# A new written-out order, split first projections and query weights loaded first, in a one-core attention and MLP block

## Chip, cores, metric

The kernel runs on one core of one Trainium2 chip. The metric is the device time in microseconds (us) of one execution. One execution was also taken with the hardware profiler; every start, duration and wait below comes from that one.

## What is computed

A transformer block over 2048 tokens of width 640. Cut to what matters:

```python
h  = x + A(layernorm(x))          # A: 32 heads of 20, in 4 segments of 512 tokens
h2 = h + B(layernorm(h))          # B: 640 -> 1728, silu, 1728 -> 640

# A, per head and segment s:
p     = softmax(q_s k_s^T * 20**-0.5 + causal mask)
a_dot = p v_s
phi   = lambda t: where(t > 0, t + 1, exp(t))
a_mem = phi(q_s) M / (phi(q_s) z + 1e-6)      # memory of the segments before s
o     = sigmoid(beta) * a_mem + (1 - sigmoid(beta)) * a_dot
M, z  = M + phi(k_s)^T v_s,  z + sum(phi(k_s))
return concat(o) @ wo
```

## The kernel before

All data lies in on-chip memory as bf16; the matrix results go to eight banks of the accumulator `ps_all`. The 32 heads are taken four at a time, in eight groups `g`; four heads of 20 rows stand at rows 0, 32, 64 and 96, and the 12 rows left between them hold the other heads, so that five projection blocks `c` (0 to 4) of 128 columns carry all of q and all of k. Groups 5 to 7 are copied out of the gaps by small transfers (`vt`, L841).

The program is a graph of named tasks, and **each task's place is written out by hand** in one long string, `ORDER`. `schedule` goes through it word by word; a word is a name, an engine after a slash where there is a choice (A ScalarE, D VectorE, S the SyncE queue), and after a colon the buffer slots that the task takes. Every engine then executes its own tasks strictly in that order, so a word that is late holds up everything behind it on its engine. Semaphore waits are derived from what each task reads and writes. Names used below:

| word | task | line | engine |
|---|---|---|---|
| `x0`.., `w_q`, `w_k`, `w_wv`, `w_w1_0`.. | load tokens or a weight | 562, 565 | SyncE or ScalarE queue |
| `n1_st`, `n1_rs`, `n1_ap` | statistics, 1/std, normalize a block of 128 tokens | 703, 712, 720 | VectorE, GpSimd, VectorE |
| `n1_tp`, `n1_te` | transpose by matmul (segment 0), its copy to `xT` | 729, 738/739 | TensorE, ScalarE/VectorE |
| `n1_tr`, `n2_tr` | transpose by DMA (later segments, and `hT`) | 744 | SyncE queue |
| `fillN` | N matmuls on zeros into an unused bank | 597 | TensorE |
| `v si`, `ve si` | values of block i in segment s, copy to `Vx` | 771, 781/782 | TensorE, ScalarE/VectorE |
| `re_wq c`, `re_wk c` | rearrange block c of a loaded weight | 675/677 | ScalarE/VectorE |
| `pr s c w`, `qe s c w` | projection c of q (w=0) or k (w=1), copy to `QK` | 805, 813/814 | TensorE, ScalarE/VectorE |
| `ex`, `ph` | exp and phi of q or k | 820, 827/830 | ScalarE, VectorE |
| `qk..`, `e..`, `mk..` | scores, their exp (two banks each), causal mask | 877, 888, 900 | TensorE, ScalarE, GpSimd |
| `av`, `oe`, `tn`, `nm`, `ad` | weights times values, copy, transpose back with the memory term, normalize, add | 923, 936/938, 952/956, 969 to 989, 997 | |
| `kt`, `mz`, `ma`, `mb` | the memory M and z | 1037, 1045, 1070 to 1081 | |
| `ot`, `wo`, `rs` | transpose the output, times wo, residual | 1098, 1106, 1114 | |
| `h1`, `th`, `s`, `h2`, `o`, `out` | MLP, second residual, store | 1130, 1138, 1144, 1162, 1172, 1176 | |

In segment 0 the first 256 tokens are scored first (`qk0x0` to `qk7x0`, two blocks), then the other 256 (`ya`, `yb`); later segments go in ticks of one group. Segment 0's MLP is in two halves, the later ones are in one.

At the start the four token blocks come in on the SyncE queue, and the three attention weights, 800 KB each, on ScalarE's queue, in the order `wv`, `wq`, `wk`. One ScalarE operation, `warm`, stands ahead of them in `ORDER`. The values take `VS = 21` columns per head, 20 and one column of ones; that constant is the same before and after.

Of the kernel before, what the change touches and what calls it, by code (L numbers as in the profile page):

```python
# [11 lines left out]
PE, AC, DV, PO, SP = "pe", "act", "dve", "pool", "sp"  # L12
# [312 lines left out]
D = 640  # L325
# [22 lines left out]
SPLIT0 = ()  # L348
# [10 lines left out]
zpad:0 warm w_wv:0 w_q:0 w_k x0:0 x1:1 x2:2 x3:3 beta mt0 mta0 mtb0 epsc iota halfc vpad1 epsg0 n1_st0:0 sel  # L359
n1_st1:2 mt1 n1_rs0 n1_ap0:0 n1_rs1 fill38:0 n1_tp0:0 n1_st2:1 n1_ap1:0 fill10:2 n1_tp1:2 n1_st3:3 n1_te0/A:0 n1_rs2  # L360
n1_rs3 n1_ap2:0 fill2:4 v00:0 n1_tp2:4 n1_ap3:1 n1_tp3:6 n1_te1/A n1_te2/D re_wq1/D:0 v01:2 n1_te3/A pr010:6 lsc0
re_wq2/D re_wk1/D:0 re_wk0/D pr011:4 re_wq0/D mt2 qe010/D:0 ve00/A:0 re_wq3/A re_wk4/D re_wk2/A pr001:0 qe001/D:0
x4/A:4,5,6,7 qe011/A zf0 ex011:0 ve01/D qk1x0:4 re_wk3/D re_wq4/D n1_st4:3 e1x0:0 pr000:1 e1x2 pr021:0 pr020:2 vpad0
lsc1 mk1x lsc2 lsc3 qe000/A qe021/A:0 ex001:1 qk0x0:4 qe020/A e0x2:1 e0x0 pr041:0 pr030:2 ex021:2 n1_st5:1 n1_st7:2
qe030/D:0 ph001:0 ph011:1 qe041/A:0 mk0x qk2x0:4 av1x:1 oe1x/D:0 e2x0:0 e2x2 pr031:3 qe031/A pr040:2 qk3x0:4 av0x:0
tn1x:1 qe040/A e3x0:1 e3x2 n1_rs5 n1_rs4 n1_rs7 v02:2 qk0yb0:4 oe0x/D:1 nm1x:0,0 n1_st6:0 ve02/D n1_ap7:1 v03:0 mt3
mta3 n1_ap5:0 mta1 mk2x n1_rs6 mk3x ve03/D ex031:0 e0yb0:0 e0yb2 fill1:2 qk1yb0:4 x8/S:8,9,10,11 w_w1_4/S:0 av2x:2
oe2x/D:0 e1yb0:1 e1yb2 w_w2_3/S:0 vt03:0 vt09 fill5:3 qk4x0:0 vt06 w_w2_0/S e4x2:0 e4x0 qk0ya0:4 e0ya0:0 e0ya2 vt00
kt00:0 w_w1_0/S vt05 vt07 vt011 vt010 vt02 n1_tr5:0 tn2x:0 v11:2 qk1ya0:4 n1_ap6:2 ph021:0 n1_tr6 vt01 vt08 ve11/A:1
n1_st8:0 n1_ap4:0 nm2x:0 av3x:0 e1ya2:1 e1ya0 v12:2 vt04 oe3x/D:0 ve12/A mk4x tn3x:0 nm3x:0 mk0yb av4x:1 n1_rs8  # L370
mk1yb qk5x0:4 n1_tr4 tn0x:0 e5x2:0 e5x0 mk5x n1_tr7 v10:2 qk6x0:4 n1_st9:3 nm0x:0 oe4x/A:1 e6x0:1 v13:0 e6x2 ve10/D
av5x:2 qk7x0:4 ve13/D kt02:1 oe5x/D:0 w_wo/S:0 ex041:2 e7x0:0 e7x2 av1y:3 mz02:0 tn5x:2 mk6x av6x:1 qk2yb0:4
ma02/A:0 e2yb0:1 e2yb2 tn4x:0 mtb1 mk7x oe1y/D:0 oe6x/A:1 nm5x:0 pr101:3 fill1:2 qk2ya0:4 e2ya2:1 e2ya0 tn6x:1
pr130:2 mm5 mk2yb mm2 qe101/D:0 nm4x:0 tn1y:0 nm6x:1 av7x:1 av0y:3 oe0y/A:0 qk3ya0:4 e3ya0:0 e3ya2 w_w2_2/S kt01:1
w_w1_1/S ph031:1 oe7x/D:1 w_w1_2/S w_w1_3/S nm1y:1 tn7x:1 nm7x:0 av2y:3 pr100:0 qk3yb0:4 n1_st11:1 n1_st10:2
oe2y/A:1 qe100/D e3yb2:1 e3yb0 ot1:0 ot0 w_w2_4/S mz01:1 pr111:3 qk4ya0:4 qe130/A:0 ma01/D:1 wo1:0 e4ya0:1 e4ya2
ph041:0 kt04:1 w_w2_1/S qe111/D:0 tn2y:3 rs1 n2_st1:4 mk3yb av3y:2 oe3y/A:1 qk4yb0:4 e4yb0:1 e4yb2 nm2y:0 n2_rs1
wo0:0 ex100:2 qk5ya0:4 tn3y:3 e5ya0:0 e5ya2 rs0 n2_st0:6 mk4yb n2_ap1:1 n2_rs0 pr121:2 mz04:0 nm3y:0 n2_ap0:0
ma04/A:2 mz00:1 qk5yb0:4 av4y:0 oe4y/D:1 ma00/D:3 e5yb0:0 e5yb2 pr141:3 qk6ya0:4 tn0y:1 ex101:0 ex111:1 n2_tr1:0
n2_tr0 pr140:0 qe141/D:0 zf1 n1_rs9 qe121/D:0 nm0y:0 e6ya2:1 e6ya0 mk5yb av5y:3 tn4y:2 n1_rs11 h1_0_6_0:1 qe140/D  # L380
ph100:0 ph111:0 oe5y/A:1 th0_6_0:0 qk6yb0:4 e6yb0:0 e6yb2 h1_0_4_0:0 pr110:3 mta2 mtb2 mzc2 mm4 s0_6_0:0 mm0 mk6yb
n1_rs10 th0_4_0:1 ex121:1 qk7ya0:4 s0_4_0 pr120:1 h1_0_1_0:0 e7ya0:0 e7ya2 nm4y:0 n1_ap9:0 h1_0_3_0:2 qe110/D
th0_1_0:1 qe120/D s0_1_0 qk7yb0:4 th0_3_0:0 h1_0_9_0:1 h1_0_11_0:0 e7yb2:1 h1_0_5_0:3 s0_3_0 th0_9_0:0 e7yb0 s0_9_0
av6y:1 qk8a0:4 th0_11_0:0 th0_5_0:1 oe6y/A:0 h1_0_0_0:2 tn6y:1 s0_5_0 epsg1 s0_11_0 e8a2:1 nm6y:0 th0_0_0:0
h1_0_7_0:3 e8a0 s0_0_0 n1_ap11:1 th0_7_0:0 h1_0_2_0:0 h1_0_13_0:1 mm9 mzc9 mzc0 qk8e0:4 mtb3 mm11 mk7yb av7y:2
s0_7_0 th0_13_0:1 s0_13_0 oe7y/D:0 e8e2:0 e8e0 h1_0_8_0:3 pr131:1 h1_0_12_0:2 th0_2_0:1 s0_2_0 qk8b0:4 th0_8_0:0
qe131/A th0_12_0:1 ph121:2 s0_8_0 n1_ap10:2 s0_12_0 h2_0_0:0 h1_0_10_0:3 h2_0_1 ex120:2 n1_ap8:3 kt03:0 n1_tr9:0
vt11:0 n1_tr11 vt16 n1_tr8 vt18 mk8a mk8e e8b0:1 e8b2 qk9a0:4 mm7 mk8b mzc11 mm3 mzc3 mm1 mzc1 th0_10_0:1 h2_0_2
tn5y:2 e9a0:0 s0_10_0 h2_0_3 e9a2 mk9a mb00:0 nm5y:0 qk9b0:4 o0 ph101:1 e9b2:0 e9b0 h2_1_0:2 av8:0 tn7y:1 qk10a0:4
oe8/A:1 e10a0:1 e10a2 nm7y:0 h2_1_1 tn8:0 h2_1_2 ph120:0 qk10b0:4 nm8:0,0 h2_1_3 vt12 vt110 vt111 kt10:1 vt19 vt10  # L390
ot3 ex141:2 e10b0:1 e10b2 o1 mk9b mm10 mzc10 mb04:0 mz03:0 ma03/D:4 qk10e0:4 ex131:0 e10e2:1 e10e0 av9:2 ph131:1 mm8
mk10b mzc7 mb01:0 mk10a mk10e ex110:0 oe9/D:1 wo3:0 qk11a0:4 e11a2:0 e11a0 mk11a mzc4 rs3 v20:2 av10:0 qk11b0:4
e11b2:1 ph110:0 ve20/D:0 e11b0 vt17 vt14 ot2 kt12:0 vt15 vt13 n1_tr10 oe10/D:0 ex130:0 mzc5 mk11b wo2:2 tn9:0
qk12a0:4 rs2 pr220:2 e12a2:1 e12a0 av11:3 qk13a0:4 oe11/A:1 nm9:0,1 pr211:0 e13a2:0 e13a0 pr200:3 qk12b0:4 ex140:1
# [59 lines left out]
def build(nc, es, A_x, A_wq, A_wk, A_wv, A_wo, A_beta, B_x, B_w1, B_w2, out):  # L454
# [109 lines left out]
    def load_w(k, dst, src, prio, bw, wr, kind="plain", engs=(SP, AC)):  # L564
        dma("w_" + k, [(W["wk"], [0])] if kind == "plain" else [], wr, lambda e: e.dma_start(out=dst, in_=src), prio, bw, kind, engs=engs)
# [666 lines left out]
```

## Time and profile before

| | |
|---|---|
| runs of the kernel before | 316.68, 314.07, 317.78, 314.02 us; median 315.37 |
| the profiled execution | 316.68 us; first to last instruction 314.9 us |
| TensorE busy | 298.2 us (95%), 2864 matmuls |
| ScalarE busy | 228.0 us (72%) |
| VectorE busy | 221.2 us (70%) |
| GpSimd busy | 144.5 us (46%) |
| DMA | 24.56 MB, mean 78 GB/s |
| granted TensorE clock, mean | 0.995 |
| matmuls on zeros (L597) | 57, 8.9 us busy |
| last matmul ends | 311.8 us |

Busy time of an engine is the union of its instructions' times. The granted clock is the share of full speed at which TensorE was allowed to run. The profiled execution's own time lies 1.78 us above its span, for what lies before the first and after the last instruction.

### The profile page before, as it was taken

What the parts mean: (1) busy time and instruction counts of PE and PEld (TensorE: products, weight loads), DVE (VectorE), ACT (ScalarE), POOL (GpSimd) and SP (SyncE); (2) the same over time, 40 slices, a digit from 0 to 9 for tenths busy, and PEclk for the clock granted to TensorE, in tenths of its full rate; (3) what the DMA queues carried; (4) which work ended last, traced back from release to release, by engine and by line L of the source; (5) the groups of instructions that cost most, each with busy time, mean ns of one, the idle gap of its engine ahead of it and who ended that gap; (6) DMA issues with size and microseconds to landing.
All of it is one profiled execution on the core that took longest, in us unless ns stands there. A gap on an engine that the chain in (4) does not pass through costs nothing.

```text
span 314.9 us, 7209 instructions
## 1 busy us (share of the span) xinstructions
PE 298.2 (95%) x2864; PEld 165.2 (52%) x2891; DVE 221.2 (70%) x489; ACT 228.0 (72%) x322; POOL 144.5 (46%) x280
## 2 busy tenths in 40 slices
PE   8799899999999989999979999999999999999995
PEld 6534454547555445565534545556554456654553
DVE  3869568777578997798879984647977495826422
ACT  3488889999899989979779998976888850005300
POOL 4328542574556773573628546434774540300000
PEclk9999799999999999999999999999999999999999
DMA  7487477440444020045563220066040004221013
GB/s 248 153 292 196 83 217 194 110 60 2 77 75 73 17 44 19 1 73 113 107 63 108 51 60 0 2 104 60 1 86 2 0 2 85 62 42 65 0 44 125
DMA packets 48353, 24.56 MB, mean 78 GB/s; under 512 B 38848, under 2 KB 47232, under 8 KB 48320
## 3 DMA queue, kind: packets, MB, share of 16 engines
q1 hardware_dynamic: 45824, 20.99, 31.0%
q10 hardware_dynamic: 2496, 3.11, 2.9%
q8 instruction: 23, 0.38, 0.5%
q14 instruction: 10, 0.08, 0.1%
HBM read 10.33 MB, written 2.62 MB: 41 GB/s over the span
## 4 chain that ended last, share of the span: by engine, by line
PE 67%; DVE 12%; ACT 10%; DMA 8%; issue 2%; POOL 0%; SPq 0%; ACTq 0%; DVEq 0%
PE ps_all L1162 18%; PE ps_all L1130 18%; PE ps_all L805 7%; PE ps_all L877 6%; PE ps_all L1106 6%; PE ps_all L923 4%; DMA x_tok<-in_A_x_dram 4%; ACT PTB L888 4%; PE ps_all L771 4%; ACT PTA L888 3%; DMA hT<-xn_rot 3%; DVE stt L703 2%; PE ps_all L952 2%; DVE xn_rot L720 1%; DVE phiQ L830 1%
## 5 line engine op out<-in xcount | busy, mean ns | idle before, releaser
L1130 PE MATMUL ps_all<-hT,w_sb 128*128 128x512 bf16 (+3 forms) x340 | 65.3, 336 | 4.0 <-DVE phiQ L827 1.8
L1162 PE MATMUL ps_all<-w_sb,sT 128*128 128x320 bf16 (+1 forms) x448 | 68.2, 300 | 0.1
L888 ACT ACTIVATE PTA<-ps_all 128x1024 bf16<-128x1024 f32 x64 | 62.2, 1026 | 6.7 <-PE ps_all L877 6.5
L1138 ACT ACTIVATE th<-ps_all 128x512 f32<-128x512 f32 (+3 forms) x70 | 34.5, 518 | 43.0 <-PE ps_all L1130 34.9
L888 ACT ACTIVATE PTB<-ps_all 128x1024 bf16<-128x1024 f32 (+1 forms) x64 | 59.0, 973 | 6.1 <-PE ps_all L877 6.0
L1144 DVE SCALAR_TENSOR_TENSOR sT<-th,ps_all 128x512 bf16<-128x512 f32 (+3 forms) x70 | 38.9, 575 | 29.9 <-ACT th L1138 29.1
L900 POOL TENSOR_SCALAR_AFFINE_SELECT PTB<-PTB 128x512 bf16<-128x512 bf16 x64 | 41.6, 650 | 34.8 <-ACT PTB L888 32.6
L1162 PEld LDWEIGHTS ps_all<-w_sb,sT 128*128 128x128 bf16 (+1 forms) x448 | 40.4, 97 | 24.4 <-issue 8.1
L1130 PEld LDWEIGHTS ps_all<-hT,w_sb 128*128 128x128 bf16 (+1 forms) x350 | 31.6, 99 | 30.6 <-issue 5.1
L888 ACT ACTIVATE PTE<-ps_all 128x1024 bf16<-128x1024 f32 (+1 forms) x40 | 35.5, 939 | 3.0 <-PE ps_all L877 2.1
L900 POOL TENSOR_SCALAR_AFFINE_SELECT PTE<-PTE 128x512 bf16<-128x512 bf16 x40 | 25.8, 646 | 21.7 <-ACT PTE L888 20.3
L703 DVE BATCH_NORM_STATS2 stt<-x_tok 128x6 f32<-128x320 bf16 x64 | 28.1, 480 | 5.9 <-DMA x_tok<-in_A_x_dram 5.5
L900 POOL TENSOR_SCALAR_AFFINE_SELECT PTA<-PTA 128x512 bf16<-128x512 bf16 x24 | 15.7, 655 | 25.3 <-ACT PTA L888 25.3
L1172 DVE SCALAR_TENSOR_TENSOR x_tok<-ps_all,x_tok 128x640 bf16<-128x640 f32 x16 | 13.2, 823 | 18.1 <-PE ps_all L1162 18.0
L771 PE MATMUL ps_all<-wv_sb,xT 128*128 128x320 bf16 x160 | 25.6, 309 | 0.2
L997 POOL TENSOR_TENSOR otok<-on 128x320 bf16<-128x320 bf16 x24 | 19.3, 810 | 11.8 <-DVE on L989 11.8
L805 PE MATMUL ps_all<-xT,wqr 128*128 128x512 bf16 x92 | 23.2, 379 | 1.5 <-issue 0.6
L1106 PE MATMUL ps_all<-wo_sb,oT 128*128 128x320 bf16 x160 | 23.9, 299 | 0.1
L805 PE MATMUL ps_all<-xT,wkr 128*128 128x512 bf16 x91 | 23.0, 380 | 0.7 <-issue 0.3
L814 DVE CAST QK<-ps_all 128x512 bf16<-128x512 f32 x24 | 16.1, 679 | 10.3 <-PE ps_all L805 10.3
L877 PE MATMUL ps_all<-QK 20*128 20x256 bf16 (+3 forms) x360 | 20.8, 288 | 2.6 <-ACT PTB L888 1.3
L712 POOL TENSOR_TENSOR rst<-mvt,eps_c 128x1 f32<-128x1 f32 x32 | 6.9, 217 | 32.0 <-DVE mvt L706 29.5
(78 smaller groups left out, 415.5 us busy)
## 6 DMA issues: line engine op xcount, KB each, us to landing
out_dram<-x_tok SPq DMA_DIRECT2D x16, 160.0 KB, 2.0
w_sb<-in_B_w_dram SPq DMA_DIRECT2D x5, 432.0 KB, 4.3
w_sb<-in_B_w_dram SPq DMA_DIRECT2D x3, 480.0 KB, 5.7
x_tok<-in_A_x_dram SPq DMA_DIRECT2D x2, 640.0 KB, 5.7
QKV<-QK SPq DMA_DIRECT2D x16, 72.0 KB
wv_sb<-in_A_wv_dram ACTq DMA_DIRECT2D x1, 800.0 KB, 5.4
sT<-in_A_wq_dram ACTq DMA_DIRECT2D x1, 800.0 KB, 8.8
sT<-in_A_wk_dram ACTq DMA_DIRECT2D x1, 800.0 KB, 10.3
```

Source lines behind the costliest of these rows:

```text
L703: T.add(DV, lambda e, hh=hh: e.bn_stats(out=stt[:, s, 6 * hh:6 * hh + 6], in_=xb[:, 320 * hh:320 * hh + 320]), reads=R((xa, xsub)), writes ...
L771: fns.append(lambda e, c=c, hh=hh: e.matmul(bank(ps, hh)[:, 0:320], lhsT=xT[:, c, 128 * i:128 * i + 128], rhs=wv_sb[:, c, 320 * hh:320 * h ...
L805: fns = [lambda e, kc=kc: e.matmul(bank(ps)[:, lo:hi], lhsT=wt[:, kc, c, :], rhs=xT[:, kc, lo:hi], start=(kc == 0), stop=(kc == NC - 1)) f ...
L877: fns.append(lambda e, j=j, o=o, r=r, q0=q0, q1=q1, qa=qa, ka=ka: e.matmul(ps_all[:, o:o + q1 - q0], lhsT=ka[32 * r:32 * r + DH, 128 * j:1 ...
L888: T.add(AC, lambda e: e.activation(out=pt[:, pta.slot, q0:q0 + 2, 0:width], in_=sc3[:, b0:b0 + 2, 0:width], func=ACT.Exp, scale=SCALE), re ...
L900: fns.append(lambda e, v=v: e.affine_select(out=v, in_=v, pattern=[[0, 4], [1, 128]], compare_op=ALU.is_ge, fill=0.0, base=0, channel_mult ...
L997: T.add(PO, lambda e: e.tensor_tensor(out=o_dst, in0=on[:, ona.slot, 0, :].rearrange("p (i x) -> p i x", i=4), in1=on[:, ona.slot, 1, :].r ...
L1106: fns.append(lambda e, c=c, hh=hh: e.matmul(bank(ps, hh)[:, 0:320], lhsT=oT[:, c, 128 * i:128 * i + 128], rhs=wo_sb[:, c, 320 * hh:320 * h ...
L1130: fns = [lambda e, c=c: e.matmul(bank(ps)[0:fw, lo:hi], lhsT=w1_sb[:, c, 128 * f:128 * f + fw], rhs=hT[:, c, lo:hi], start=(c == 0), stop= ...
L1138: T.add(AC, lambda e: e.activation(out=th[0:fw, tha.slot, lo:hi], in_=bank(ps)[0:fw, lo:hi], func=ACT.Tanh, scale=0.5), reads=R((ps, [0])) ...
L1144: T.add(DV, lambda e: e.scalar_tensor_tensor(out=sT[0:fw, f, lo:hi], in0=th[0:fw, tha.slot, lo:hi], scalar=1.0, in1=bank(ps)[0:fw, lo:hi], ...
L1162: fns.append(lambda e, f=f, fw=fw, hh=hh: e.matmul(bank(ps, hh)[:, 0:320], lhsT=sT[0:fw, f, 128 * i:128 * i + 128], rhs=w2_sb[0:fw, f, 320 ...
```

## The change

Three edits; there is no new function.

1. `SPLIT0 = (0, 1)`: in segment 0 the projections of blocks 0 and 1, of q and of k, are done as two halves of 256 tokens, `pr..x` and `pr..y`, each with a copy of its own (`qe..x`, `qe..y`). Each half needs just two of the four transposed token blocks. Ten matmuls of 256 columns take the place of five of 512, in four projections.
2. On ScalarE's queue the weights are loaded in the order `wq`, `wk`, `wv`, behind the same `warm`.
3. `ORDER` is a new string: all words stand again, nearly all in other places, with other slots and often other engines for copies.

```diff
-SPLIT0 = ()
+SPLIT0 = (0, 1)
...
-zpad:0 warm w_wv:0 w_q:0 w_k x0:0 x1:1 x2:2 x3:3 beta mt0 mta0 mtb0 epsc iota halfc vpad1 epsg0 n1_st0:0 sel
-n1_st1:2 mt1 n1_rs0 n1_ap0:0 n1_rs1 fill38:0 n1_tp0:0 n1_st2:1 n1_ap1:0 fill10:2 n1_tp1:2 n1_st3:3 n1_te0/A:0 n1_rs2
-n1_rs3 n1_ap2:0 fill2:4 v00:0 n1_tp2:4 n1_ap3:1 n1_tp3:6 n1_te1/A n1_te2/D re_wq1/D:0 v01:2 n1_te3/A pr010:6 lsc0
-re_wq2/D re_wk1/D:0 re_wk0/D pr011:4 re_wq0/D mt2 qe010/D:0 ve00/A:0 re_wq3/A re_wk4/D re_wk2/A pr001:0 qe001/D:0
-x4/A:4,5,6,7 qe011/A zf0 ex011:0 ve01/D qk1x0:4 re_wk3/D re_wq4/D n1_st4:3 e1x0:0 pr000:1 e1x2 pr021:0 pr020:2 vpad0
...
+zpad:0 warm w_q:0 w_k mt0 epsg0 halfc iota x0:0 x1:1 x2:2 x3:3 beta w_wv:0 mt2 mta0 mta2 sel n1_st0:0 mt1 n1_st1:2
+n1_st2:1 mtb2 epsc n1_rs0 n1_rs1 n1_rs2 n1_ap1:0 n1_ap0:1 fill49:0 n1_tp1:0 n1_st3:2 n1_rs3 mta1 vpad1 n1_te1/A:0
+re_wq1/D:0 n1_ap2:0 n1_tp0:2 n1_te0/A fill9:4 pr010x:2 n1_ap3:1 re_wq0/A re_wk1/D:0 n1_tp2:0 pr000x:3 n1_tp3:4
+pr011x:6 lsc0 re_wk0/D n1_te3/D pr001x:7 re_wk4/D n1_te2/A pr001y:4 qe001y/D:0 re_wk2/A qe001x/A re_wq3/D re_wk3/D
+mt3 mtb1 lsc1 qe011x/A:0 vpad0 v01:0 pr000y:4 lsc2 qe000y/D pr021:6 re_wq2/A mm3 x4/S:4,5,6,7 ex001:0 qe010x/A
+re_wq4/D zf0 qe021/A:0 qe000x/A pr020:2 ve01/D:0 qk0x0:4 e0x2:0 pr011y:0 qe011y/A e0x0 pr010y:1 qe010y/A lsc3
+n1_st4:2 pr041:3 n1_st6:1 n1_st7:0 qe020/A mk0x qk1x0:4 ex021:1 e1x2:1 v00:0 ve00/D pr031:2 w_wo/S:0 x8/S:8,9,10,11
...
-    load_w("wv", wv_sb[:, :, :], cw(A_wv), -97, 5.9, [(W["wv"], [0])], "fix", (AC,))
-    load_w("q", wraw[:, 0, :, :], cw(A_wq), -99, 7.5, [(sT0, ["q"])], "fix", (AC,))
-    load_w("k", wraw[:, 1, :, :], cw(A_wk), -98, 9.0, [(sT0, ["k"])], "fix", (AC,))
+    load_w("q", wraw[:, 0, :, :], cw(A_wq), -99, 5.9, [(sT0, ["q"])], "fix", (AC,))
+    load_w("k", wraw[:, 1, :, :], cw(A_wk), -98, 7.5, [(sT0, ["k"])], "fix", (AC,))
+    load_w("wv", wv_sb[:, :, :], cw(A_wv), -97, 9.0, [(W["wv"], [0])], "fix", (AC,))
```

Further places in the new string that are spoken of below: the matmuls on zeros are 49, 9, 1, 3 and 5 (before 38, 10, 2, 1, 5 and 1); `fill1`, `fill3` and `fill5` stand around `qk0ya0`; `mz00` stands ahead of `v11`; `w_w1_3`, `w_w1_0` and `w_w1_1` stand behind `ot1` or `ot0` on the SyncE queue, and `w_w1_4` is on ScalarE's queue; the last word of matrix work is `h2_14_3` (before `h2_13_3`), and nine of the sixteen stores stand in the string behind `h2_14_3`. `x4` goes to the SyncE queue (before on ScalarE's).

## The prediction

> **What bounds the kernel now.** I read the page first, then the busy time by stage, then the timeline and the chain of waits at the places where TensorE was not busy.
>
> ```profile
> span 314.9 us, 7209 instructions
> PE 298.2 (95%) x2864; PEld 165.2 (52%) x2891; DVE 221.2 (70%) x489; ACT 228.0 (72%) x322; POOL 144.5 (46%) x280
> PEclk9999799999999999999999999999999999999999
> ...
> L597 PE MATMUL ps_all<-zpad 128*128 128x256 bf16 x57 | 8.9, 315 | 1.1 <-DVE zpad L570 1.1
> ```
>
> TensorE is busy 95% of the span, so the time is the matrix work, which no edit removes, plus what TensorE loses by waiting, by matmuls on zeros and by a lower clock. Only those can change. The clock row has one 7, in the slice from 31.5 to 39.4 us. By stage (columns: window, its length, busy us of TensorE, of its weight loads, VectorE, ScalarE, GpSimd, granted clock, DMA share, GB/s):
>
> ```profile
> 0.00:10.00 10.00, 7.87 (x60) 6.16 (x61) 4.74 (x15) 3.02 (x4) 4.28 (x20) 1.00 0.78 256
> 20.00:25.00 5.00, 4.95 (x43) 1.96 (x42) 3.61 (x14) 4.73 (x8) 2.31 (x6) 1.00 0.70 209
> 30.00:35.00 5.00, 3.53 (x49) 1.73 (x48) 4.56 (x12) 4.55 (x7) 2.17 (x4) 1.00 0.46 113
> 35.00:40.00 5.00, 5.00 (x45) 2.50 (x43) 1.19 (x5) 3.83 (x6) 3.81 (x7) 0.66 0.50 95
> 46.00:75.00 29.00, 27.10 (x334) 14.71 (x340) 22.29 (x63) 27.75 (x46) 15.57 (x36) 1.00 0.48 106
> 157.70:252.50 94.80, 91.94 (x909) 47.45 (x916) 68.66 (x138) 80.14 (x104) 51.28 (x85) 1.00 0.27 45
> ```
>
> Four readings. The first 10 us hold almost no useful matrix work. From 30 to 35 TensorE stands idle 1.5 us, and right after it the clock is 0.66. From 46 to 75 ScalarE is busy 27.75 of 29 us, more than TensorE: there the exps set the pace. From 158 on TensorE does, and ScalarE has 15% to spare. The timeline at the first two places:
>
> ```profile
> 10.01 1.52 PE L771 MATMUL ps_all<-wv_sb,xT 128*128 128x320 bf16 x10
> 17.45 0.34 PE L877 MATMUL ps_all<-QK 20*128 20x256 bf16 x8
> 17.85 1.51 ACT L888 ACTIVATE PTE<-ps_all 128x768 bf16<-128x768 f32 x2
> 32.02 2.54 SPq L744 DMA_TRANSPOSE xT<-xn_rot  x2
> 34.64 2.23 PE L771 MATMUL ps_all<-wv_sb,xT 128*128 128x320 bf16 x10
> 42.54 1.52 PE L771 MATMUL ps_all<-wv_sb,xT 128*128 128x320 bf16 x10
> ```
>
> The values come first (10.01), the first scores at 17.45, the first exp at 17.85. At 34.64 `v11` has waited for its DMA transpose; its ten matmuls take 2.23 us where ten at 42.54 (`v13`) take 1.52.
>
> **The change, part by part.** Two things that its short name suggests are not in it: the 21 value columns are there before (`VS` is not touched), and `warm` stands ahead of the weight loads in both orders. Cost: nothing. What remains is the load order, the split and the string.
>
> *Zeros.* 67 matmuls in place of 57. Late in the first group they follow each other every 0.11 us: 10 x 0.11 = +1.1 us of TensorE, but 11 more stand in the first group, which ends near 8.3 us and is hidden behind the wait for the first normalized block (9.5).
>
> *Split.* Four projections of 5 x 512 (1.09 us each between starts) become eight of 5 x 256 (0.56, from the segment-0 MLP matmuls): +0.1 us in all. Four copies of 512 columns (0.60 on ScalarE, 0.68 on VectorE) become eight of 256. No such copy is in the trace; below it stands half of 0.60, above it the 256-column copy with a scale, 0.48 (L936). I take 0.36: +0.5 us over two engines, bounds 0 to +1.4.
>
> *Load order.* From issue to landing: `wv` 5.4, `wq` 8.8, `wk` 10.3 us, issued at 1.11, 1.60 and 2.17, so the three places land near 6.5, 10.4 and 12.5. All are 800 KB; I give the places to the new owners. `wq` is there at 6.5, but VectorE takes it up only behind the statistics of three blocks: stats of block 2 start when it lands (7.99), then two normalizations of 0.40, stats of block 3, and `re_wq1` ends near 11.3.
>
> *The start, walked along the new lists with these rows.* Transposes 9.5 to 10.4 (block 1 first); copies to `xT` on ScalarE (0.70 each) to 11.4; `pr010x` 11.5; six halves and `v01`, each ready when its turn comes, to 17.05; `pr021` and `pr020` (1.09 each) to 19.25; `qk0x0` waits for `qe000x` on ScalarE, 19.35. First exp 19.75, **1.9 us later than before**, with 8.4 us of useful matrix work done against 7.6. Net +1.1 us.
>
> *From there to `v13`.* Exps (0.75 between the starts of two) and copies go on as ScalarE reaches them; TensorE waits 0.4 us at 27.6 and 0.25 at 32.0. `fill1`, `mz00`, `fill3` and `fill5` fill the place where before TensorE stood idle. `v11` waits as before for its transpose: nine `vt` of 0.7 us precede it on SyncE's queue, five of them behind the last copies of q and k (28.5), so it is issued near 32.1 and used near 35.05 (34.64 before). Useful work by then: 22.4 against 22.1. Then `v11`, `v10`, `v12` at 1.47 with scores between, and **`v13` at 41.45 against 42.54**. Useful work before `v13`: 28.2 against 28.0. So TensorE has lost 13.25 us by then in place of 14.54: **-1.3 us**. That includes the clock: the stretch at half speed from about 35.2 to 38.6 cost two blocks of values and the scores between them about 1.7 us, half of its 3.4, and I count this as saved, since TensorE in my walk is busy some 90% of 31 to 35.
>
> A row and a rule differ here. The longest wait of TensorE ahead of the drop was 1.01 us, in a stretch in which it was busy 1.16 of 1.5 us and then 0.49 of 1.5. The Trainium skill (TensorE: Matmul & The Clock Gate, HAM oscillation) says to avoid idle gaps of over some 3.4 us, by which nothing would have dropped here; the trace decides. The same page (Part 1) says that the window is free-running, so that the same program can be hit or spared by chance; by that the 1.7 us are no property of either order, and the sum would be 317.1.
>
> *The rest.* From `v13` on the useful matrix work, entry by entry of either list at its row's interval (projection 1.09, block of values or of `wo` 1.47, MLP 1.10 and 1.17 or 0.87, scores 0.17 or 0.24), is 256.2 us before and 256.1 after. Before, the last matmul ends at 311.77, so 269.2 us went by: 13.0 lost. I take the same loss after. Bounds: -3.7 (first rival) and +3.8 (second rival). At the step from segment 3's `wo13` to `h1_3`, the chain residual, statistics, 1/std, normalize, transpose took 6.8 us (272.2 to 279.05), covered by 8.16 us of MLP matmuls; after, 7.3 us stand there: still covered, 0; without cover it would cost up to 6.8. The last two stores have seven others ahead of them on SyncE's queue; `o13`, which frees them, ends 5.3 us before the last matmul, and seven issues at 0.43 take 3.0: 0, bound +0.5.
>
> *Other steps moved on queues.* `w1_3`, `w1_0`, `w1_1` go behind `ot1` and `ot0` on SyncE's queue (issued 51.9 to 55.4 before) and `w1_4` behind ScalarE's exps near 60. With 4.3 us to landing they are there by 65; the MLP starts near 67 to 68 with its own wait for `hT` (66.7 before). 0; if one came 3 us late, TensorE would wait 2, since everything behind `h1_0_12_0` is held.
>
> Sum: 316.68 (the profiled run) - 1.3 + 0 = **315.4 us**. The median of the four runs is 315.37; two of them at 314.0 may well be without the clock drop. So: no change.
>
> **Rivals.** *First, faster.* From 46 to 75 the exps set the pace, and the new string has 58.9 us of useful matrix work ahead of `qk8a0`, against 55.2, beside the same 63 us of ScalarE work. If TensorE gets these 3.7 us done in the exps' shadow and keeps the lead, 315.4 - 3.7 = **311.7**. For it: 27.3 us of matrix work fit into 29. Against: TensorE already is busy 27.1 of those 29, so there is little shadow left.
>
> *Second, slower: ScalarE is behind later.* At the same matrix work (end of segment 0's MLP, 157.7 us before) the new string has 138.9 us of ScalarE work done against 143.2. From there to the last weights-times-values (252.5 before) ScalarE has 87.9 us to do in place of 84.5. If its pace there (84.5 in 94.8 us) can't rise, because scores wait for banks and banks for exps, this takes 94.8 x 87.9 / 84.5 = 98.6: +3.8, **319.2 us**. It decides as soon as ScalarE's busy share in that stretch can't go above the 85% it had. For it: a walk by hand shows single waits poorly, and each late entry holds all behind it. Against: 15% to spare.
>
> *Third, the clock.* The drop comes all the same, in the start or elsewhere: 315.4 + 1.7 = **317.1 us**.
>
> **How the numbers follow.** Forecast 0.34, first rival 0.26, second 0.32, third 0.08. The likeliest is 315.4, with 313.5 to 317.3 as its own range. About 1% is what a measurement of this kernel can tell from no change (its runs span 1.2%). Faster by over 1% is below 312.2: the first rival, 0.26. Slower is above 318.5: the second, 0.32. Within: 0.34 + 0.08 = 0.42. The range goes down to the first rival less a further 1.2 (a third of the 3.8 by which the runs of before differ), and up to the second with the clock drop on top (319.2 + 1.7): 310.5 to 321.0.
>
> **What would show it.** First score at 19.35 and first exp at 19.75; `v13` near 41.5; no slice of the clock row below 9; 67 matmuls on zeros; ScalarE near 85% in the stretch that was 158 to 252; last matmul near 310.5. I am wrong if TensorE's idle time after 42 us differs by over 3 us from before: above, if waits for exps in segments 2 and 3 have grown; below, if `qk8a0` comes by 74 us with the matrix work ahead of it done.

## The result, and the profile after

The new order takes 315.98 us (median of 43 runs, 315.14 to 317.76), the old one beside it 314.51 (69 runs, 313.06 to 318.62): ratio 1.0040, 95% interval 1.0029 to 1.0051. It is slower by 0.4%, within the 1% of "no change". Its profiled execution took 314.98 us, below all 43 of these runs, with a span of 313.2 us; that of the old order, 316.68, was one of the slower ones. So the two profiles stand in the wrong order, and what a typical run loses has to come from the traces of the experiments.

The page of the changed kernel, the clock row and the matmuls on zeros (from the groups by line):

```profile
PE 296.6 (95%) x2894; PEld 167.7 (54%) x2921; DVE 223.5 (71%) x494; ACT 226.9 (72%) x321; POOL 143.7 (46%) x280
PEclk9999999999999999999999999999999999999999
```

```profile
L597 PE MATMUL ps_all<-zpad 128*128 128x256 bf16 x67 | 9.5, 302 | 1.1 <-DVE zpad L570 1.1
```

The 7 in the clock row is gone, and the zeros are 67. The changed kernel by stage (columns as before):

```profile
30.00:35.00 5.00, 4.34 (x53) 2.47 (x51) 4.27 (x13) 5.00 (x8) 4.63 (x10) 1.00 0.43 77
35.00:40.00 5.00, 4.72 (x53) 2.62 (x51) 4.11 (x10) 3.47 (x6) 3.67 (x7) 1.00 0.41 79
46.00:75.00 29.00, 26.59 (x355) 14.62 (x354) 23.56 (x63) 27.38 (x42) 16.69 (x42) 1.00 0.57 154
157.70:252.50 94.80, 92.05 (x917) 47.96 (x923) 68.39 (x138) 81.58 (x106) 51.99 (x86) 1.00 0.24 48
```

From 30 to 35 TensorE is busy 4.34 us (3.53 before) and the clock stays at 1.00. From 46 to 75 it was busy 0.5 us less than before, not more. In the last stretch ScalarE is busy 86%. The timeline at the same places as before:

```profile
15.80 1.52 PE L771 MATMUL ps_all<-wv_sb,xT 128*128 128x320 bf16 x10
19.96 0.34 PE L877 MATMUL ps_all<-QK 20*128 20x256 bf16 x8
20.36 0.81 ACT L888 ACTIVATE PTE<-ps_all 128x768 bf16<-128x768 f32 x1 [0.50 <-PE ps_all L877]
35.65 1.53 PE L771 MATMUL ps_all<-wv_sb,xT 128*128 128x320 bf16 x10
42.18 1.52 PE L771 MATMUL ps_all<-wv_sb,xT 128*128 128x320 bf16 x10
305.81 4.28 PE L1162 MATMUL ps_all<-w_sb,sT 128*128 128x320 bf16 x28
```

The values now come behind five of the halves (`v01` at 15.80). The first scores come at 19.96, `v11` at 35.65, `v13` at 42.18, and the last matmul ends at 310.09 (311.77 before).

### The profile page after: what moved, and what is told of

It is laid out like the page before. It is cut to its first block, busy times and chain, and to the rows that moved or that the text cites. A ratio compares the mean times of both kernels' runs of the same rounds, so it can differ in the third digit from the quotient of the medians.

```text
span 313.2 us, 7298 instructions
## 1 busy us (share of the span) xinstructions
PE 296.6 (95%) x2894; PEld 167.7 (54%) x2921; DVE 223.5 (71%) x494; ACT 226.9 (72%) x321; POOL 143.7 (46%) x280
## 4 chain that ended last, share of the span: by engine, by line
PE 61%; ACT 12%; DVE 8%; DMA 7%; SPq 4%; POOL 3%; issue 3%; ACTq 0%; DVEq 0%
PE ps_all L1130 18%; PE ps_all L1162 15%; PE ps_all L805 9%; PE ps_all L877 6%; ACT PTE L888 4%; ACT PTA L888 4%; PE ps_all L1106 4%; PE ps_all L923 3%; ACT PTB L888 3%; DMA hT<-xn_rot 3%; PE ps_all L771 3%; SPq L841 2%; DMA x_tok<-in_A_x_dram 2%; PE ps_all L952 2%; DVE stt L703 2%
## 5 line engine op out<-in xcount | busy, mean ns | idle before, releaser
L1162 PE MATMUL ps_all<-w_sb,sT 128*128 128x320 bf16 (+1 forms) x448 | 67.4, 300 | 0.0
L1138 ACT ACTIVATE th<-ps_all 128x512 f32<-128x512 f32 (+1 forms) x70 | 34.4, 518 | 40.2 <-PE ps_all L1130 36.9
L1144 DVE SCALAR_TENSOR_TENSOR sT<-th,ps_all 128x512 bf16<-128x512 f32 (+1 forms) x70 | 38.9, 576 | 30.6 <-ACT th L1138 29.7
L900 POOL TENSOR_SCALAR_AFFINE_SELECT PTB<-PTB 128x512 bf16<-128x512 bf16 x64 | 40.8, 638 | 35.2 <-ACT PTB L888 33.0
L805 PE MATMUL ps_all<-xT,wqr 128*128 128x512 bf16 (+1 forms) x102 | 23.4, 359 | 1.7 <-issue 0.8
L771 PE MATMUL ps_all<-wv_sb,xT 128*128 128x320 bf16 x160 | 24.5, 300 | 0.0
L805 PE MATMUL ps_all<-xT,wkr 128*128 128x512 bf16 (+1 forms) x100 | 23.1, 359 | 1.2 <-issue 0.3
L814 DVE CAST QK<-ps_all 128x512 bf16<-128x512 f32 (+1 forms) x27 | 17.9, 666 | 8.3 <-PE ps_all L805 7.8
L877 PE MATMUL ps_all<-QK 20*128 20x256 bf16 (+3 forms) x360 | 20.6, 285 | 2.2 <-ACT PTE L888 0.7
L989 DVE TENSOR_TENSOR on<-ps_all,rd 128x640 bf16<-128x640 f32 x24 | 19.8, 824 | 0.8
```

What stands on the lines that cost most here:

```text
L771: fns.append(lambda e, c=c, hh=hh: e.matmul(bank(ps, hh)[:, 0:320], lhsT=xT[:, c, 128 * i:128 * i + 128], rhs=wv_sb[:, c, 320 * hh:320 * h ...
L805: fns = [lambda e, kc=kc: e.matmul(bank(ps)[:, lo:hi], lhsT=wt[:, kc, c, :], rhs=xT[:, kc, lo:hi], start=(kc == 0), stop=(kc == NC - 1)) f ...
L877: fns.append(lambda e, j=j, o=o, r=r, q0=q0, q1=q1, qa=qa, ka=ka: e.matmul(ps_all[:, o:o + q1 - q0], lhsT=ka[32 * r:32 * r + DH, 128 * j:1 ...
L900: fns.append(lambda e, v=v: e.affine_select(out=v, in_=v, pattern=[[0, 4], [1, 128]], compare_op=ALU.is_ge, fill=0.0, base=0, channel_mult ...
L989: T.add(DV, lambda e: e.tensor_tensor(out=on[:, ona.slot, :, :].rearrange("p b (x e) -> p b x e", e=DH), in0=v[:, :, :, 0:DH], in1=r2.unsq ...
L1138: T.add(AC, lambda e: e.activation(out=th[0:fw, tha.slot, lo:hi], in_=bank(ps)[0:fw, lo:hi], func=ACT.Tanh, scale=0.5), reads=R((ps, [0])) ...
```

## The experiments

There were four sessions on four chips, each with the old order beside the others on the same chip. Its median there was 314.22, 315.05, 315.21 and 314.60, so a kernel is compared by its ratio or with its neighbours of one session. Each run's mean granted clock shows whether the clock dropped in it: 0.995 or lower with a drop. Only a trace shows where in the run the drop lies, and one run of each kernel has a trace (two of the old order). Kernels with a shorter string have line numbers 3 lower (L874 for L877). "Front" is the order up to `qk7x0`, near 46 us.

**Session 1: which part of the change.** `e1` takes the front of the old order, with its loads and whole projections, and the new order behind it; nine buffer slots had to be chosen anew, and 19 words that the new order has ahead of `qk7x0`, and the old one has not, stand at the seam.

```diff
-zpad:0 warm w_q:0 w_k mt0 epsg0 halfc iota x0:0 x1:1 x2:2 x3:3 beta w_wv:0 mt2 mta0
...
-ex041:0 mk1yb mk5x av5x:6 mtb3 qk7x0:0
+zpad:0 warm w_wv:0 w_q:0 w_k x0:0 x1:1 x2:2 x3:3 beta mt0 mta0
...
+e6x0:1 v13:0 e6x2 ve10/D av5x:2 qk7x0:4
```

> The old string up to qk7x0 (the last scores of segment 0's first 256 tokens, some 46 us into the run; no split, wv loaded first), then the new string's order for all that is left, with nine slots given anew. Theory A (the 0.4% are lost at the start: the new front issues its first scores 2.5 us later, at 19.96 against 17.45, and reaches v13 at 42.2 where the old one without its clock drop would be near 40.8): as fast as the kernel before, 314.5, ratio 0.997 to 1.002. Theory B (the loss is in the later order, ScalarE behind in segments 2 and 3): as slow as the changed kernel, 316.0, ratio 1.003 to 1.006.

Measured: 314.68 us (12 runs), ratio 1.0006 (0.9982 to 1.0030). Beside it `e3`, which is the new order but for one load, took 315.48. So the new front costs 0.8 us, although `e1` pays for its seam: from 45 to 50 us TensorE is busy 3.34 us there (3.98 in the changed kernel). By the range that it was given, theory A holds. But the intervals of the two ratios overlap, and `e1`'s ten runs without a drop, at 314.75, lie 0.7 above those of the old order, 314.01: of the 1.3 us between `e3` and the old order, the front has the larger part, and the order behind it or the seam may have the rest. (The two runs with a drop take 314.68.)

`e2` is the reverse: new front, old order behind it.

```diff
-e6x0:1 v13:0 e6x2 ve10/D av5x:2 qk7x0:4
+ex041:0 mk1yb mk5x av5x:6 mtb3 qk7x0:0
```

> The new string up to qk7x0 (split, wq and wk loaded first), then the old string's order for the rest, with six slots given anew. Theory A (start): 316.0, ratio 1.003 to 1.006. Theory B (later order): 314.5, ratio 0.997 to 1.002. If both hybrids are slower than both kernels, the seam itself costs, and neither theory is decided.

Measured: 323.57 us, ratio 1.0297 (1.0255 to 1.0339). Its stages behind the seam:

```profile
46.00:48.00 2.00, 0.28 (x10) 0.11 (x2) 1.83 (x7) 1.69 (x3) 0.76 (x3) 1.00 1.24 354
48.00:50.00 2.00, 0.88 (x21) 0.65 (x22) 0.00 (x0) 0.03 (x1) 1.86 (x4) 1.00 0.33 27
50.00:52.00 2.00, 2.00 (x24) 0.77 (x22) 0.92 (x3) 1.35 (x3) 0.78 (x2) 0.63 0.28 65
```

TensorE stands still for 2.8 of 4 us, and the clock falls to 0.63. I laid this to four weight loads that stand at 40.3 us ahead of two transposes on SyncE's queue. `e7` below shows that they were not the main cause.

`e3` is the new order with the loads in the old order, `wv` first.

```diff
-zpad:0 warm w_q:0 w_k mt0 epsg0 halfc iota x0:0 x1:1 x2:2 x3:3 beta w_wv:0
+zpad:0 warm w_wv:0 w_q:0 w_k mt0 epsg0 halfc iota x0:0 x1:1 x2:2 x3:3 beta
```

> The changed kernel with the three weights in the old load order wv, wq, wk, nothing else. In the profile after, wq is first used at 10.72 and wk at 12.91; in the old places they would land near 10.4 and 12.5. Theory (the load order is no part of the difference, it is hidden behind the normalization of the first blocks): within 0.2 us of the changed kernel, ratio to before 1.003 to 1.006, first scores still near 20.0. Rival (the new order needs the early wq): first scores 1 to 2 us later, about 317, ratio 1.007 to 1.011.

Measured: 315.48 us, 1.0029 (1.0009 to 1.0050), with first scores at 19.93 and `v13` at 42.14: no part of the difference that shows here lies in the load order.

`e4` is the new order without the split; the whole projections stand where the second halves stood.

```diff
-SPLIT0 = (0, 1)
+SPLIT0 = ()
```

> The changed kernel without the split: pr000, pr001, pr010 and pr011 whole, each in the place of its second half; the words of the first halves are gone. Theory (the first halves fill TensorE from 11.3 to 15.2, while blocks 2 and 3 are still being normalized and copied): without them TensorE stands idle there, the four halves of 0.56 us come later, so first scores 1 us later and v13 2 us later: 317.5 to 318, ratio 1.008 to 1.012. Rival (ScalarE sets the pace from the first exp on, and four copies fewer on it and VectorE give the time back): 316, ratio 1.003 to 1.006.

Measured: 318.37 us, 1.0126 (1.0089 to 1.0164), 2.9 us above `e3`. Its first scores come at 20.94 and `v13` at 44.05 us, 1.0 and 1.9 later than in the new order: its first whole projection starts at 15.17, behind a wait of 1.77 us for the copy of the last token block, where the first half started at 11.31. (Three of its six runs had the clock drop, which is told below; the three others take 317.8.) So the split is worth 2 to 3 us to an order made for it.

**Session 2: the clock drop, and a clean old kernel.**

```diff
-fill1:0 qk0ya0:4 ve03/A tn1x:0 fill3:1 av2x:2 mz00:3 nm1x:0,0 oe2x/D:1 e0ya2:0 ma00/D:0 fill5:1 qk4x0:0
+qk0ya0:4 ve03/A tn1x:0 av2x:2 mz00:3 nm1x:0,0 oe2x/D:1 e0ya2:0 ma00/D:0 qk4x0:0
```

> The new order without nine of its ten added zero matmuls, those between 30 and 34 us. Theory Z (the clock drop at 35 us comes when TensorE is about half busy for 2 us before it, and these zeros prevent it): the granted clock falls below 0.997 in at least 2 of the runs, these take about 317.4 us, the others 315.9 as the new order with its zeros does. Rival (the zeros only fill time in which TensorE waits, and the new order is free of the drop for its other placements): no run below 0.997, the median between 315.0 and 316.0 us.

Measured: 316.87 us. Five of 12 runs have the drop (median 318.29), seven have not (316.37); the old order beside it, 316.15 and 314.61. As theory Z says, without these zeros the drop comes back. In the new order with all its zeros none of 44 runs had it, the profiled one among them, nor any of the 24 of `e3` and `e9`; in the old order 36 of 92. The traced run of `e5` is one without a drop, so that it lies at 35 us in the five others is likely and not shown.

`e6` puts zeros into the old order.

```diff
-vt06 w_w2_0/S e4x2:0 e4x0 qk0ya0:4 e0ya0:0 e0ya2
+vt06 w_w2_0/S e4x2:0 e4x0 fill2:4 qk0ya0:4 e0ya0:0 e0ya2
...
-vt011 vt010 vt02 n1_tr5:0 tn2x:0 v11:2
+vt011 vt010 vt02 n1_tr5:0 fill6:0 tn2x:0 v11:2
```

> The old order with eight zero matmuls put where TensorE waits between 32.6 and 34.3 us: two ahead of the scores qk0ya0, six ahead of the transposes tn2x. Theory Z: no run has a granted clock below 0.997 and the median is that of the old order's undropped runs, 314.0 us (313.7 to 314.4), while about 3 in 10 runs of the old order beside it have the drop and take 315.4. Rival (the drop comes from something other than this wait): about 3 in 10 of its runs still have the drop, median 314.2 or higher.

Measured: 315.89 us, 1.0031 (1.0004 to 1.0058). The drop came in 1 of 12 runs, against 10 of 23 beside it: theory Z had none, its rival some 4. The time did not come down. The timeline of TensorE shows why:

```profile
33.14 0.39 PE L594 MATMUL ps_all<-zpad 128*128 128x256 bf16 x2
34.93 0.83 PE L594 MATMUL ps_all<-zpad 128*128 128x256 bf16 x6 [1.01 <-ACT PTE L885]
```

The six zeros need a bank, all eight are taken, and they wait 1.01 us for the exp that frees one, just as the transposes behind them did. They fill nothing and stand on the path. Undropped runs take 315.77, 1.16 above the old order's; the zeros' 0.83 us is the part of it that the trace shows.

`e7` is `e2` with those weight loads held back.

```diff
-mtb3 qk7x0:0 mtb0 w_w1_4/S:0 w_w2_3/S w_w2_0/S w_w1_0/S n1_st8:5
+mtb3 qk7x0:0 mtb0 n1_st8:5
...
-e3ya0:0 e3ya2 kt01:1 w_w1_1/S
+e3ya0:0 e3ya2 kt01:1 w_w1_4/S:0 w_w2_3/S w_w2_0/S w_w1_0/S w_w1_1/S
```

> The new order up to and with the scores qk7x0, the old order after it, and four weight loads (w1 rows 4 and 0, w2 blocks 3 and 0) held back until behind the transposed keys kt01, so that they no longer stand ahead of kt02 on the DMA queues. Theory A (the new order loses its time in the stretch before 46 us): about 315.9 us, 1.9 over the undropped old order. Theory B (it loses it in the rest): about 314.2 us. If the seam still costs more than 1 us of TensorE time between 44 and 54 us, it can't tell the two apart.

Measured: 327.43 us. From 46 to 48 us TensorE is still busy only 0.47, and in both runs the wait that ends near 48.2 us (1.80 and 1.81) is one for an exp, so the loads were not what stopped it there; from 48 to 50 it is busy 1.51 in place of 0.88. Held back, the seven loads go out at 50.56 us ahead of `ot1` and `ot0`, for which TensorE then waits 3.27 us at 63. The question of A or B stays without an answer from this side.

`e8` is the old kernel once more, for its trace: 315.44 us, clock 1.00 throughout.

> The kernel before once more, for a profile without the clock drop: in 7 of 10 cases about 314.0 us with clock 1.00 in every slice, and the last values projection v13 at 40.9 us, 1.7 earlier than in the profile with the drop. If theory A holds, the new order is then behind it by about 1.3 us at v13 (42.18) and by between 1 and 2 us at the last matmul. If theory B holds, the lead at v13 is as large but the old kernel gives it back until 160 us, and the new order's loss comes later.

The expectation was missed: `v13` at 42.82, no earlier than with the drop (42.54). VectorE, then TensorE in `e8`:

```profile
22.84 0.89 DVE L703 BATCH_NORM_STATS2 stt<-x_tok 128x6 f32<-128x320 bf16 x2 [2.69 <-DMA x_tok<-in_A_x_dram]
26.47 0.64 DVE L814 CAST QK<-ps_all 128x512 bf16<-128x512 f32 x1
```

```profile
27.16 1.25 PE L805 MATMUL ps_all<-xT,wqr 128*128 128x512 bf16 x5 [1.81 <-DVE QK L814]
```

Here another loss took the place of the drop. VectorE waits 2.69 us for token rows 4 to 7; a QK copy is queued behind its statistics, and TensorE waits 1.81 us for the bank that the copy frees. In the profile of before the same load ended the wait of VectorE at 21.48 us, and TensorE lost nothing. In `e1` and `e6`, which share the old front up to there, the same wait of TensorE is 1.17 and 0.56 us. So the old front has two losses that come by chance, and `v13` near 42.5 is no sign of a clean run.

The traces also differ later, mostly where TensorE meets a transpose by DMA. The new order first (its own profile, then `e3`, then `e5`, which share its order from 46 us on):

```profile
160.76 1.03 PE L1130 MATMUL ps_all<-hT,w_sb 128*128 128x512 bf16 x4 [1.02 <-DMA hT<-xn_rot]
```

```profile
160.94 1.25 PE L1127 MATMUL ps_all<-hT,w_sb 128*128 128x512 bf16 x5 [0.68 <-DMA hT<-xn_rot]
236.87 1.25 PE L1127 MATMUL ps_all<-hT,w_sb 128*128 128x512 bf16 x5 [0.84 <-DMA hT<-xn_rot]
```

```profile
161.57 1.25 PE L1127 MATMUL ps_all<-hT,w_sb 128*128 128x512 bf16 x5 [1.27 <-DMA hT<-xn_rot]
266.61 1.53 PE L1103 MATMUL ps_all<-wo_sb,oT 128*128 128x320 bf16 x10 [1.15 <-DMA oT<-otok]
```

The waits at 237 and 267 are not in the changed kernel's own profile, its fastest run. They are what slower runs can have on top: the traced runs of `e3` (316.09) and `e5` (317.09) lie 0.6 and 0.7 us above the medians of their kind, so how often such a wait comes is not shown. SyncE's queue ahead of the first and the last of them, in the new order and in `e5`:

```profile
151.94 3.94 SPq L744 DMA_TRANSPOSE hT<-xn_rot  x3
155.93 0.58 SPq L1176 DMA_DIRECT2D out_dram<-x_tok  x1
156.56 2.50 SPq L744 DMA_TRANSPOSE hT<-xn_rot  x1
```

```profile
259.80 3.84 SPq L1095 DMA_TRANSPOSE oT<-otok  x3
263.68 1.72 SPq L1173 DMA_DIRECT2D out_dram<-x_tok  x1
265.45 1.23 SPq L1095 DMA_TRANSPOSE oT<-otok  x1
```

Both times an output store, for which TensorE does not wait, stands between the transposes. In a row they take 1.3 us each on the queue; the one behind the store took 2.50, and in `e5` the store itself 1.72 (0.58 in the new order's own profile, which doesn't wait at 267). The queue is not the whole story: at 161 us in `e5` the transpose behind the store took 1.21 on the queue, and TensorE waited longest, 1.27.

**Session 3: the stores, and the late tokens.**

```diff
-e19a2 ma14 out2 o3 n2_tr5 mk19a
+e19a2 ma14 o3 n2_tr5 out2 mk19a
...
-s2_11_0 out4 out7 ad31 ot15:0 wo15:6 ot14 rs15 n2_st15:0 n2_rs15 ot12 out6 wo14:4
+s2_11_0 ad31 ot15:0 wo15:6 ot14 rs15 n2_st15:0 n2_rs15 ot12 wo14:4
...
-n2_ap13:3 n2_tr13 o9
+n2_ap13:3 n2_tr13 out4 out7 out6 o9
```

> The new order with four output stores put behind transposes on SyncE: out2 behind n2_tr5 (rows of hT for the second hidden-layer group), and out4, out7, out6 behind n2_tr13. Theory S (the new order's typical run is some 1.4 us above the old one because TensorE waits for transposes that stand behind output stores: 0.7 to 1.3 us for hT at 161 us and, in some runs, 1.15 us for oT at 267): the wait at 161 falls below 0.5 us, the one at 267 is gone, and the median falls by 0.7 to 1.3 us, to about 315.0 where the new order takes 315.9 on the same chip. Rival (the transposes are late because the norms that feed them are): both waits stay, median within 0.3 us of the new order's.

Measured: 314.96 us (12 runs, 11 of them below 315.7), ratio 0.9999 (0.9969 to 1.0029). SyncE's queue and TensorE in `e9`:

```profile
152.10 5.26 SPq L741 DMA_TRANSPOSE hT<-xn_rot  x4
157.41 2.09 SPq L1173 DMA_DIRECT2D out_dram<-x_tok  x2
```

```profile
160.46 1.03 PE L1127 MATMUL ps_all<-hT,w_sb 128*128 128x512 bf16 x4 [0.56 <-DMA hT<-xn_rot]
```

The fourth transpose starts at 156.09 in place of 156.56, and the wait is down from 1.02 to 0.56 us, a little above theory S's "below 0.5". There is none at 237 or 267, but neither is there in the new order's own profile. In the new order the norm that feeds this transpose ends at 155.78, and the store goes out first; in `e9` the norm ends at 155.94 and the transpose follows at once. So the store held it back by some 0.6 us. The rest of the wait is another's: the transpose landed 4.1 us after its start (3.9 in the new order, 4.4 in `e5`; the median of the four is 2.8), and why is not shown.

The median stands against the old order's as 0.9999 where the new order had 1.0040 and `e3` 1.0029; against the old order's runs without a drop, `e9` stands 0.7 us higher and `e3` 1.5. So the four moved stores are worth some 0.8 to 1 us, as theory S said. The interval just touches that of the new order and overlaps that of `e3`, so the size is likely rather than shown.

```diff
-re_wk2/A pr001:0 qe001/D:0 x4/A:4,5,6,7 qe011/A
+re_wk2/A pr001:0 qe001/D:0 x4/S:4,5,6,7 qe011/A
```

> The old order with one word changed: the load of token rows 4 to 7 (x4) is issued by SyncE ahead of x8 and two weight loads, as the new order does, and no longer by ScalarE beside them. Theory X (in the old order x4 lands at 21.5 to 22.8 us, VectorE waits for it with a QK copy queued behind, and TensorE waits 0 to 1.8 us at 26 us for that copy; that is what spreads the old order's runs): x4 lands by 20 us, that wait is 0, v13 ends some 1.5 us earlier than in the profile of e8 (42.8), and the median falls by 0.5 to 1.5 us, unless a later wait for a transpose (xT at 102, hT at 116 and 161 us) takes it back, in which case it stays within 0.3 us of the old order's.

Measured: 314.85 us, 0.9989 (0.9960 to 1.0017), with 312.48 as the fastest run of any kernel here. The profiled run of `e10` on VectorE, and by stage:

```profile
20.31 0.86 DVE L700 BATCH_NORM_STATS2 stt<-x_tok 128x6 f32<-128x320 bf16 x2
```

```profile
30.00:35.00 5.00, 3.56 (x49) 1.78 (x47) 4.90 (x13) 4.55 (x8) 2.24 (x4) 0.93 0.63 152
35.00:40.00 5.00, 4.94 (x49) 2.52 (x51) 0.86 (x4) 3.78 (x6) 3.89 (x8) 0.73 0.44 83
```

VectorE no longer waits for the tokens (20.31 in place of 21.48 to 22.84), and TensorE no longer for the copy. `v13` comes at 42.40, with the drop ahead of it. The load on ScalarE's queue at 14.51 us shared the DMA engines with `x8` and two weight loads that SyncE issued from the same moment on; on SyncE's queue it goes ahead of them. The Trainium skill (DMA: Bandwidth & Descriptors, Issuing engines are not separate DMA queues) has the rule behind this row: loads from different issuing engines run on the same hardware engines. But most of the gain is given back: `e10` has the drop in 8 of 12 runs, the old order beside it in 13 of 29. Those of `e10` take 315.1, the others 313.8, and the old order's 316.0 and 314.3. So each kind of run is 0.5 to 0.9 us faster and the dearer kind comes more often, a possibility that the expectation did not have. One that it had shows too: the traced run waits 0.97 us for `xT` at 102.

`e11` joins both: old front with `x4/S`, new order behind it, the stores as in `e9`.

> The old order up to the scores qk7x0 with x4 issued first by SyncE, the new order after it, with the four stores behind transposes as in the run before. If theories S and X both hold, this is the fastest of all: about 313.5 us, 0.5 to 1 below the old order. If the front's gains are taken back later (TensorE arrives earlier and waits longer for hT at 161 us), it stays at e1's 314.7, ratio 1.00.

Measured: 314.43 us, 0.9975 (0.9946 to 1.0004), 0.5 below `e9`; 8 of 12 runs have a drop. The four others take 313.4 to 314.3, with a median 1.2 below that of `e9`, none of whose runs has one. Seven of the eight have a lower mean clock (0.987 to 0.994) than most dropped runs of the old order (0.995), so their drop is longer or there are two; where it lies is not recorded. The traced run has none:

```profile
40.94 1.52 PE L768 MATMUL ps_all<-wv_sb,xT 128*128 128x320 bf16 x10
```

```profile
30.00:35.00 5.00, 3.56 (x50) 1.83 (x49) 4.93 (x12) 4.55 (x7) 2.18 (x5) 1.00 0.57 137
```

`v13` at 40.94 is the old front with neither of its two losses, 1.2 us ahead of the new front's 42.18. And from 30 to 35 us TensorE is busy 3.56 us, as in `e10`, which has the same front, but the clock stays at 1.00 where it fell there.

**Session 4.** `e12` adds zeros to `e11`.

```diff
-e4x2:0 e4x0 qk0ya0:4 e0ya0:0
+e4x2:0 e4x0 fill2:4 qk0ya0:4 e0ya0:0
...
-vt02 n1_tr5:0 tn2x:0 v11:2
+vt02 n1_tr5:0 fill3:0 tn2x:0 v11:2
```

> The kernel of the run before (old order up to qk7x0 with x4 first, new order after it, four stores behind transposes) with five zero matmuls added where TensorE waits for ScalarE: two ahead of the scores qk0ya0, in a wait of 0.2 to 0.3 us, three ahead of the transposes tn2x, where they cost some 0.4 us of TensorE time. Theory Z: the clock drop, in 8 of 12 runs of the kernel without them, comes in at most 2 of 12, and the runs gather about that kernel's undropped 313.8 us plus 0.4, at 314.2, with ratio 0.996. Rival (five are too few, or the drop has another cause): the drop stays in half of the runs or more, and the median is 314.8 or higher.

Measured: 314.22 us, 0.9983 (0.9950 to 1.0015). The drop came in 3 of 12 runs, one more than expected and fewer than the 8 of 12 without these zeros. The undropped runs take 314.18, near the 314.2 worked out, but on another chip, where the old order's undropped runs take 313.95 (314.30 beside `e11`): by these the zeros cost 0.7 us and not 0.4. No kernel of this study is shown to be faster than the old one; `e11` and `e12` come nearest.

## Why the prediction was right

**No change, 315.4: right in the total, by terms that partly cancel.** The two edits that the prediction sets aside, the 21 value columns and `warm`, are the same before and after, and cost nothing. In the profiled run, 314.98, the front gained 0.7 us less than said and the rest lost 1.2 us less; that these errors point in opposite ways is luck. The median, 315.98, came 0.6 above the forecast.

**The front: too kind by 0.7 us.** `v13` was put at 41.45 and came at 42.18. It is 0.36 us earlier than before, with 0.2 us more useful work done by then, so the term of -1.3 measured -0.6; the 0.7 us lie in the walk. `pr010x` was in time (11.31 against 11.5), but only five of the six halves are done ahead of `v01` at 15.80; the sixth stands behind it, two waits of 0.19 and 0.27 us fall between the first ones, and the first scores come 0.6 us late (19.96 against 19.35). From there to `v13` the walk lost 0.1 more: the transpose for `v11` was issued at 33.03 in place of 32.1, and `v11` came at 35.65 in place of 35.05. The 256-column copy, put at 0.36 us, took 0.37 to 0.38 on ScalarE and 0.42 on VectorE.

**The base of the front was not clean.** The prediction took the drop, 1.7 us, as the one loss of the old front that chance can spare. `e8` shows the late tokens as a second one (1.81 us of TensorE), `e11` what is left without both (`v13` at 40.94). Against that the new front is 1.2 us behind. Swapping it moved the median by 0.8 us (`e1` against `e3`) or 0.5 (`e11` against `e9`), and by 1.2 where `e11`'s runs with a drop are left out.

**The clock.** Right that it would be gone, and the runs speak for its reason, TensorE's work from 31 to 35 us (busy 3.55 of these 4 us, near the 90% of the walk): with the zeros 0 of 44 runs, without them 5 of 12. The price of 1.7 us fits: dropped runs of the old order stood 1.4, 1.5, 1.7 and 2.9 us above the others in the four sessions, though the others may hold the late tokens; in `e10`, which has no late tokens, it was 1.3. The prediction held against itself that chance decides. The Trainium skill (TensorE: Matmul & The Clock Gate, Part 1) calls the window free-running; that fits with 36 of 92 runs of one program, and with `e10` and `e11`, equal from 30 to 35 us but for the clock. But the order sets the odds, from 0 of 44 to 8 of 12.

**The rest: "the same loss, 13.0 us".** From `v13` to the last matmul the changed kernel's profile took 310.09 - 42.18 = 267.9 us, so with 256.1 of useful work it lost 11.8. But this run lies 1.0 below the median: if a typical one loses that behind `v13`, it loses about 12.8 there, and the term was good for it. That `v13` came at 42.14 to 42.44 in the traces of `e3`, `e5` and `e9` supports this; it is not shown for the changed kernel's own typical runs. What made it up was not seen: the prediction walked the chain to `h1_3` and found it covered, and did not walk those to the second and third hidden-layer groups and to the last `wo`, where TensorE waits 0.7 to 1.3 us at 161 and in some runs 0.6 to 1.2 us at 237 or 267 for transposes, two of them behind stores. The old order can have such a wait too: 1.78 us at 161 in the profile of before, where the fourth transpose starts at 157.2 and lands 4.6 us later (the profile names an operation on VectorE), but only 0.20 in `e8`. The sign by which the prediction would have called itself wrong did not come: from 42 us to the last matmul TensorE's idle time is 9.0 us in both profiles. The last stores themselves cost nothing, as said: the last matmul ends 3.1 us ahead of the span's end in both orders.

**The rivals.** The first needed `qk8a0` by 74 us; it came at 75.76 (74.51 before), with TensorE busy less from 46 to 75: no shadow was used. Its 3.7 us were also too many. Counted in the two strings, the words of matrix work ahead of `qk8a0` differ by one projection (`pr131`, 1.09) and the split's 0.1; from `v13` to `qk8a0` TensorE is busy 30.90 us against 29.96. The second needed a ScalarE that cannot go above 85% from 158 us on; it went to 86% and the last weights-times-values came at 251.53 (251.80 before). Of the 3.4 us that it moved there, 1.4 came (81.58 us busy against 80.14). Its pace was not worked out from the share it names either: 84.5 us in 94.8 would be 89%, the busy time is 80.14. The third, a drop all the same, did not come.

**The comparison.** The forecast was set against a profiled run of 316.68 and a median of four. With 69 runs the old order's median is 314.51, 0.9 lower; this makes up 0.9 of the 1.5 us between the two medians, and the forecast's own error (315.98 against 315.4) the other 0.6.

## What to carry to other kernels

When a profile is one run out of a spread of 1% or more, take the trace of a second run before costing a change of that size: the waits that differ between two traces of one kernel are the ones to look at first for what separates its runs. On a queue that issues in order, put stores that TensorE does not wait for behind the transposes that it needs next, and a load that is needed first ahead of the bulk loads on the same queue. Zero matmuls for the clock were paid for where all banks were taken (`e6`, `e12`): put them where a bank is free while TensorE waits.

## What the runs showed of the hardware

The clock fell to half with no long pause of TensorE: in the profile of before it had been busy 3.53 of 5 us, and this was the longest wait:

```profile
34.32 0.25 PE L956 MATMUL ps_all<-ident,oTs 128*128 128x84 bf16 x2 [1.01 <-ACT PTE L888]
```

The same stretch need not bring the drop: from 31.5 to 34.5 us TensorE was busy 1.61 of 3 us in `e10`, which dropped, and 1.61 in `e11`, which did not. In the kernels with four or more runs of each kind, those with a drop took 0.9 (`e11`) to 2.9 us (old order, session 4) longer than those without one.

With the tokens in time (`e10`, `e11`) 16 of 24 runs had a drop, with the old order's load of them 36 of 92. A wait of 0.6 to 1.8 us at 26 us, as the late tokens bring it (`e6`, `e1`, `e8`), seems to make the drop less likely. Why was not tried.
